# Six tiles of the attention result turned by a 16-bit-plane DMA in place of TensorE, in a fused attention and MLP block

## The chip, the cores and the metric

The kernel runs on one core of a Trainium2 chip. The metric is the device time of one execution in microseconds, lower being better. Times are given as the median of several runs. Beside them there is one profiled execution, whose span is somewhat shorter than the time, since the time also holds what lies around the span.

## The reference

One transformer block on a sequence of 2048 rows of 512 numbers, in float32. The first half is layer norm, one product that gives q, k and v, attention of 32 heads of 16 numbers over a dilated local window (row s looks at rows s, s-2, ..., s-14), and a product with `wo`. The second half is layer norm and an MLP with a hidden layer of 1792, whose activation is the square of relu.

```python
x = A_x
h = x + attention(layernorm(x) @ wqkv) @ wo          # 32 heads, window 8, dilation 2
n = layernorm(h)
r = maximum(n @ w1 + b1, 0)
out = h + (r * r) @ w2 + b2
```

## The kernel before

**Precision.** TensorE multiplies in a reduced float32 form. To keep float32's accuracy, each operand is split in a high part (`hi`, a rounding copy on ScalarE, line 141) and a low part (`lo`, the difference, line 144, on VectorE or GpSimd), and each product is made of three: high by high, low by high, high by low. `mm3` (line 224) issues them as 12 matmuls of 512 columns.

**Tiles and passes.** A tile is 128 rows by 512 numbers. There are 16 tiles, in four groups of four; tile t is in group t // 4. Two neighbouring tiles share one attention output `o_t[s]`, s = t // 2, a buffer of 128 x 2 x 512 out of three that have the tag "o". A first phase makes q, k and v of all tiles and attention and `wo` of group 0. Then the main loop makes three passes, u = 0, 1, 2. In each, TensorE does the MLP of group u, in slots p = 0 to 16: `mlp1` of hidden block p (12 matmuls, line 224), then `mlp2` of the block three slots back (line 808). Into the same slots go the steps of the next group: transposes of the attention result, the `wo` product, and transposes of the normed h. After the loop the MLP of group 3 runs in another form (line 731).

**The order around the change.** The order is written out by hand. Tables at the head of the file give the slot in which each of the four tiles of the next group has its steps; in the third pass the last two tiles are one slot earlier:

```python
LH = 3, 4, 10, 11     # load h
OP = 6, 7, 12, 13     # o_T: transpose the attention result
WP = 8, 9, 13, 14     # the wo product
HP = 15, 15, 16, 16   # h_T: transpose the normed h
```

What a slot starts on TensorE is issued first. Then `end_slot` runs the chores that are due (`at(0, ...)` is due in this slot, `at(1, ...)` in the next), then lets attention run on (`pump`), then runs the late chores (`after`). Each engine takes its instructions in this order. All loads and stores are issued by SyncE, in one queue, and a transfer that must wait holds up those behind it.

**Attention** is a generator, `stream`, which issues VectorE's products and sums (lines 335, 346, 369) and GpSimd's sums over the window, the last of which writes `o` (line 403). It reads windows of k and v (line 243) and q (line 256) from HBM, loaded two steps ahead. `pump` issues attention until the estimated VectorE time has caught up with the estimated TensorE time; `pump(until=s)` issues it until `o_t[s]` is complete.

**The steps of a tile.** `o_T(t)` pumps until its attention is complete, has TensorE transpose four 128x128 blocks into a PSUM bank (`transposes`, line 199), and puts the high part `oh` on ScalarE and the low part `ol` on VectorE among the chores of the same slot. For the third tile of a group both lie in one buffer `ohl` with the tag "o"; otherwise each is a "row", one of 15 buffers that h, r, rl, hn, raw weights and others share. `wo_product(t)` uses `oh` and `ol`, and puts four steps behind itself: the sum with h and its statistics on VectorE (`h_add`, line 577) in the same slot, then the norm on ScalarE, the bias on GpSimd (line 587) and the spill of h to HBM, one to three slots later.

In the loop there are two PSUM banks, taken in turn, for `mlp1`, `wo` and transposes alike. ScalarE empties the bank of `mlp1` with the first step of `hidden` (line 784), a chore of the slot after.

Of the kernel before, what the change touches and what calls it, by code (L numbers as in the profile page):

```python
# [7 lines left out]

F32 = mybir.dt.float32
F32R = mybir.dt.float32r  # L10
AF = mybir.ActivationFunctionType
ALU = mybir.AluOpType
X = mybir.AxisListType.X
# [2 lines left out]
P = 128  # L16
KB = D // P
FB = F // P
R = 4
RI = 2  # L20
# [7 lines left out]
NEG = -4.0e9  # L28
ROWS = 15
LAG = 3  # L30
SLOW = 1.01, 1.12, 1.08
DELAY = 3
WJ = 2
# [1 line left out]
OT = 4, 5, 10, 12  # L35
WO = 7, 9, 13, 15
HT = 20, 20, 21, 23
W2 = (18,)
LH = 3, 4, 10, 11
OP = 6, 7, 12, 13  # L40
WP = 8, 9, 13, 14
HP = 15, 15, 16, 16
UP = 14, 14, 15, 15
HL = (14, 0), (14, 1), (15, 0), (15, 1)
# [8 lines left out]
def block_kernel(ctx, tc, x, wqkv, wo, w1, b1, w2, b2, out):  # L53
    nc = tc.nc
# [3 lines left out]
    att = ctx.enter_context(tc.tile_pool(name="att", bufs=2))  # L58
# [27 lines left out]

    big_h = wpool.tile([P, 3 * KB, D], F32R, name="big_h")
    big_l = wpool.tile([P, 3 * KB, D], F32R, name="big_l")
    wq_h, wq_l = [t.rearrange("p (k c) n -> p k (c n)", k=KB) for t in (big_h, big_l)]
    wo_h = wpool.tile([P, KB, D], F32R, name="wo_h")  # L90
    wo_l = wpool.tile([P, KB, D], F32R, name="wo_l")
    w1_h = wpool.tile([P, KB, F], F32R, name="w1_h")
    w1_l = wpool.tile([P, KB, F], F32R, name="w1_l")
    w2_h, w2_l = {}, {}

    def row(name, shape=(P, D), dt=F32):
        return work.tile(list(shape), dt, name=name, tag="row", bufs=ROWS)
# [8 lines left out]
    def at(delta, fn, *a):  # L106
        due.setdefault(now["slot"] + delta, []).append((fn, a))
# [61 lines left out]
    def act_stats(key, src):  # L169
# [4 lines left out]
        scrap = row("scrap")  # L174
        nc.scalar.activation(scrap, src, AF.Identity, accum_out=nm[:, 0:1])
        nc.scalar.activation(nm[:, 1:2], nm[:, 0:1], AF.Identity, scale=-1.0 / D)
# [30 lines left out]
    def hi_T(tr, h_dst):  # L207
        for d, src in parts(tr, h_dst):
            hi(d, src)

    def lo_T(tr, h_dst, l_dst):
        for (d, src), h in zip(parts(tr, l_dst), h_dst):
            lo(nc.vector, d, src, h)
            dve(0.16 + 0.53 / len(h_dst))
# [16 lines left out]
    o_t = {}  # L231
# [177 lines left out]
    def pump(until=None):  # L409

        while (done[until] < G) if until is not None else (now["dve"] < now["pe"]):
            todo = sums[:]
            sums.clear()
            t = next(stream, "end")
            for a in todo:
                add_up(*a)
            if t == "end":
                now["dve"] = 1e9
                return
            if t is None:  # L420
                now["dve"] = max(now["dve"], now["pe"])
                return
            dve(t * SLOW[min(now['sub'] + 1, 2)])

# [126 lines left out]
    hs, hn = {}, {}  # L551
    oT = {}
# [9 lines left out]
    def o_T(t):  # L562
        s, j = divmod(t, RI)
        pump(until=s)
        tr = transposes(o_t[s][:, j, :])
        if t % R == RI:

            ohl = att.tile([P, 2, KB, P], F32R, name="ohl", tag="o", bufs=3)
            oT[t] = ohl[:, 0], ohl[:, 1]
        else:  # L570
            oT[t] = row("oh", (P, KB, P), F32R), row("ol", (P, KB, P), F32R)
        at(0, hi_T, tr, [oT[t][0]])
        at(0, lo_T, tr, [oT[t][0]], [oT[t][1]])

    def h_add(t, ps):
        h = hs[t]
        nc.vector.tensor_tensor(out=h, in0=ps, in1=h, op=ALU.add)
        dve(0.7)
        norm_stats(t, h)
# [16 lines left out]
    def wo_product(t, slots):  # L596
# [4 lines left out]
        for n, (fn, a) in zip(slots, ((h_add, (t, ps)), (h_norm, (t,)), (add_b2, (t,)),  # L601
# [5 lines left out]
    hh, hl = [[big_l[:, n:n + 2].rearrange("p k (i c) -> p k i c", i=R) for n in ns]  # L607
              for ns in ((0, 3), (6, 9))]

    def h_T(t):  # L610
        if t // R == R - 1:
            return last_h_T(t)
        tr = transposes(hn.pop(t), "mm")
        i = t % R
        hs_, ls_ = [a[:, :, i] for a in hh], [a[:, :, i] for a in hl]
        if len(turn["mm"].tags) > 2:
            at(0, hi_T, tr, hs_)
        else:
            due.setdefault(now["slot"], []).insert(0, (hi_T, (tr, hs_)))
        at(0, lo_T, tr, hs_, ls_)  # L620
# [7 lines left out]
    last_tr, banks = {}, {}  # L628
# [260 lines left out]
    for n in range(16):  # L889
        gp, t = divmod(n, 4)  # L890
# [27 lines left out]
    def first_phase(t0):  # L918
        def chores(m):
            if t0 + 3 < 16:  # L920
                if m in (0, 2):
                    at(0, x_stats, t0 + 2 + m // 2)

                early = t0 == 12
                if m + early in (6, 7):
                    at(0, x_norm, t0 - 4 + m + early)
                if m in XT[early]:
                    x_T(t0 + 2 + XT[early].index(m))
            if t0 + 5 < 16 and m in (6, 9):
                at(0, load_x, t0 + 2 + m // 3)  # L930
            if jobs and m % 3 == 0:
                at(0, weight_job)
            k = t0 // 2 * 12 - 72 + m
            if k == 19:
                dve(HOLD)
            for t in range(R):
                if k == OT[t]:
                    at(0, load_h, t)
                    o_T(t)
                if k == WO[t]:  # L940
                    wo_product(t, (1, 3, 4, 6))
                    now["pe"] += 2.73
                if k == HT[t]:
                    h_T(t)
            if k in W2:
                at(0, load_w2, W2.index(k))

        def half(m):
            end_slot(1.37)
            chores(m)  # L950

        for n in range(6):
            chores(2 * n)
            qkv_of(t0 + n % 2, n // 2, lambda: half(2 * n + 1))
            end_slot(1.37)
# [41 lines left out]
    for u in range(R - 1):  # L997
        now["sub"] = u
        first, end = u == 0, False
        fs = list(range(FB)) if first else [*sorted(place), 12, 13]  # L1000
        fs += [f for f in range(12) if f not in fs and (u < 2 or f not in ENDS)]
        fs += ENDS if u == 2 else []
        need = [] if first else [f for f in fs if f < 12 and f not in place]
        acc = [psum.tile([P, D], F32, name="acc", tag=tag) for tag in ("acc0", "acc1", "tr0", "tr1")]
        js = range(R)


        todo, halves = {}, {}
        for i in js:
            t = R * (u + 1) + i  # L1010
            if not end:
                a = i // 2 if u == 2 else 0
                for p, *what in ((LH[i] - a, at, 0, load_h, t), (OP[i] - a, o_T, t),
                                 (WP[i] - a, wo_product, t, (0, 1, 2 + 3 * a, 3 + 3 * a))):
                    todo.setdefault(p, []).append(what)
                p, h = (HP[i], i % 2) if u < 2 else HL[i]
                (todo, halves)[h].setdefault(p, []).append((h_T, t))
            todo.setdefault(UP[i], []).append((at, 0, unspill, R * u + i))
        if u == 2:
            for p, *what in ((12, at, 0, t_load, 0), (12, at, 0, t_load, 1), (13, after, 0, t_sums, 0),  # L1020
                             (13, after, 0, t_sums, 1), (13, at, 1, t_split, 0),
                             (14, after, 0, t_split, 1)):
                todo.setdefault(p, []).append(what)

        def half(p):
            run(due)
            for fn, *a in halves[p]:
                fn(*a)

        for p in range(FB + LAG):  # L1030
            more = 0.0
            if p == FB:
                run(due)
                dve(HOLD)
            if u < 2 and p == FB - 2:
                dve(HOLD)
            for fn, *a in sorted(todo.get(p, []), key=lambda x: x[0] is wo_product):
                fn(*a)
                more += 2.73 if fn is wo_product else 0.0
            if p < FB:  # L1040
                mlp1(u, fs[p])
                more += 2.73
                if first:
                    at(0, split_w2, p)
                    if p + 1 < FB:
                        load_w2(p + 1)
            q = p - LAG
            if q >= 0:
                f = fs[q]
                mlp2(u, f, acc, js, q == 0, q == FB - 1,  # L1050
                     (lambda: half(p)) if p in halves else None)
                more += 2.74
                if f < 12 and (need or first and p < FB - LAG):
                    free.append(place.pop(f))
                    if need:
                        at(1, fetch, need.pop(0))
            end_slot(more)
        for i in js:
            at(u // 2, finish, R * u + i, acc[i])
# [48 lines left out]
    h = hs[S // P - 1]  # L1108
# [34 lines left out]
```

## Time and profile before

| | |
|---|---|
| time, median of 3 runs | 514.47 us (514.29 to 515.16) |
| the profiled execution: its span | 513.0 us |
| TensorE matmul busy | 506.4 us, 99% |
| VectorE busy | 376.7 us, 73% |
| GpSimd busy | 350.0 us, 68% |
| ScalarE busy | 256.2 us, 50% |
| first phase | 0 to about 160 us |
| main loop, three passes | about 160 to 436 us |
| the last group's MLP | about 436 to 513 us |

Times in profile lines are microseconds from the start of the span unless they are marked as nanoseconds. PE is TensorE, PEld its weight loads, DVE is VectorE, ACT is ScalarE, POOL is GpSimd and SPq is SyncE's queue. In a line of a timeline stand start, duration, engine, line, operation, output and input with their shapes, the number of instructions, and in brackets the idle time before it and what ended it. A group's line ends with its busy time, the mean of one instruction in nanoseconds, and the idle time before. A line of waits has the total, how often, and the longest. A line of DMA issues has the count, the size, and the median time from issue to landing.

### The profile page before, as it was taken

The page shows a single profiled execution, that of the slowest core. Times are in us where ns is not written, and L with a number is a line of the kernel's source. Part 1 is how long each engine was busy: PE and PEld are TensorE (multiplying, and loading weights), DVE is VectorE, ACT ScalarE, POOL GpSimd, SP SyncE. Part 2 cuts the span into 40 slices and gives each one's busy share as a digit, 9 for nine tenths or more (in the row PEclk, how much of TensorE's full clock was granted, in tenths as well). Part 3 has the DMA queues.
Part 4 walks back from the last instruction along what each step waited for, and adds up shares of the span by engine and source line. Part 5 has one row for each costly group of instructions (what it writes and reads, how often), then busy time and mean ns, then how long its engine had stood idle before and what let it go on. Part 6 is the DMA issues. An engine that isn't in the chain of part 4 may idle for free.

```text
span 513.0 us, 7625 instructions
## 1 busy us (share of the span) xinstructions
PE 506.4 (99%) x2508; PEld 429.3 (84%) x2508; DVE 376.7 (73%) x524; ACT 256.2 (50%) x498; POOL 350.0 (68%) x430
## 2 busy tenths in 40 slices
PE   7999999999999999999999999999999999999997
PEld 6999788888888888888888888888888888989996
DVE  5489799988998798976889799778984035742333
ACT  4634687767424763463364334336432525666542
POOL 4714888894885895896778759676889544685520
PEclk9999999999999999999999999999999999999999
DMA  9677989889677895685487537557632352454112
GB/s 265 193 221 188 271 283 315 275 274 278 196 234 201 291 299 173 175 232 180 129 266 229 163 94 231 174 160 257 219 94 65 106 159 84 142 145 145 63 41 82
DMA packets 88239, 97.37 MB, mean 190 GB/s; under 512 B 8328, under 2 KB 56712, under 8 KB 88200
## 3 DMA queue, kind: packets, MB, share of 16 engines
q1 hardware_dynamic: 87256, 96.37, 61.4%
q10 hardware_dynamic: 944, 0.52, 0.3%
q8 instruction: 19, 0.31, 0.3%
q14 instruction: 20, 0.16, 0.1%
HBM read 72.65 MB, written 24.25 MB: 189 GB/s over the span
## 4 chain that ended last, share of the span: by engine, by line
PE 92%; POOL 3%; DMA 2%; DVE 1%; issue 1%; ACT 1%; SPq 0%; POOLq 0%; ACTq 0%
PE mm L224 45%; PE acc L808 29%; PE wo L224 9%; PE mm L731 6%; PE tr L199 4%; DMA wraw<-in_A_wqkv_dram 1%; DMA qkv_d<-y 1%; POOL pr L403 1%; POOL h L587 1%; POOL tl L144 0%; PE half L831 0%; SPq L432 0%; POOL wo_l L144 0%; DVE pr L346 0%; DVE ex L369 0%
## 5 line engine op out<-in xcount | busy, mean ns | idle before, releaser
L403 POOL TENSOR_TENSOR pr<-pr 128x512 f32<-128x512 f32 (+1 forms) x128 | 132.1, 1032 | 51.2 <-DVE pr L346 45.7
L224 PE MATMUL mm<-big_l,w_h 128*128 128x512 f32 x336 | 89.5, 392 | 0.0
L346 DVE TENSOR_TENSOR pr<-ex,v 128x1024 f32<-128x1024 f32 x64 | 78.0, 1221 | 11.6 <-POOL o L403 7.6
L335 DVE TENSOR_TENSOR pr<-qp,k 128x1024 f32<-128x1024 f32 x64 | 76.8, 1201 | 5.7 <-ACT qp L264 5.7
L369 DVE TENSOR_REDUCE ex<-pr 128x64 f32<-128x1024 f32 x64 | 78.4, 1225 | 1.8
L224 PEld LDWEIGHTS mm<-big_l,w_h 128*128 128x128 f32 x336 | 62.3, 188 | 12.8 <-DVE ol L144 0.2
L144 POOL TENSOR_TENSOR rl<-r,rh 128x512 fp32r<-128x512 f32 x42 | 55.4, 1318 | 22.5 <-ACT rh L141 22.4
L224 PE MATMUL mm<-big_h,xl 128*128 128x512 f32 (+1 forms) x208 | 55.9, 379 | 0.2 <-DVE xl L144 0.2
L224 PE MATMUL mm<-big_h,xh 128*128 128x512 f32 (+1 forms) x208 | 53.5, 378 | 0.7 <-ACT xh L141 0.7
L784 ACT ACTIVATE r<-mm,b_sb 128x512 f32<-128x512 f32 x42 | 28.8, 686 | 47.9 <-PE mm L224 46.1
L224 PE MATMUL mm<-big_l,xh 128*128 128x512 f32 (+1 forms) x208 | 52.7, 375 | 0.0
L808 PE MATMUL acc<-big_l,rh 128*128 128x512 f32 x190 | 52.7, 391 | 0.0
L808 PE MATMUL acc<-big_h,rh 128*128 128x512 f32 x190 | 52.3, 392 | 0.0
L808 PE MATMUL acc<-big_h,rl 128*128 128x512 f32 x190 | 51.8, 390 | 0.0
L493 ACT COPY y<-mm 128x512 f32<-128x512 f32 (+1 forms) x52 | 28.6, 552 | 40.0 <-PE mm L224 30.1
L224 PE MATMUL mm<-big_l,w_l 128*128 128x512 f32 x168 | 45.0, 390 | 0.0
L224 PEld LDWEIGHTS mm<-big_h,xh 128*128 128x128 f32 x208 | 37.6, 188 | 7.0 <-ACT xh L141 1.7
L224 PEld LDWEIGHTS mm<-big_l,xh 128*128 128x128 f32 x208 | 38.2, 188 | 6.0
L224 PEld LDWEIGHTS mm<-big_h,xl 128*128 128x128 f32 x208 | 37.2, 188 | 5.7 <-DVE xl L144 0.6
L808 PEld LDWEIGHTS acc<-big_h,rl 128*128 128x128 f32 x190 | 35.7, 188 | 7.5
L808 PEld LDWEIGHTS acc<-big_l,rh 128*128 128x128 f32 x190 | 35.4, 188 | 7.3
L808 PEld LDWEIGHTS acc<-big_h,rh 128*128 128x128 f32 x190 | 34.8, 188 | 6.5
(148 smaller groups left out, 879.8 us busy)
## 6 DMA issues: line engine op xcount, KB each, us to landing
k<-qkv_d SPq DMA_DIRECT2D x48, 288.0 KB, 2.8
v<-qkv_d SPq DMA_DIRECT2D x48, 288.0 KB, 4.0
qkv_d<-y SPq DMA_DIRECT2D x18, 512.0 KB, 4.3
big_l<-w2l_d SPq DMA_DIRECT2D x24, 256.0 KB, 3.1
xt<-in_A_x_dram SPq DMA_DIRECT2D x16, 256.0 KB, 4.3
q<-qkv_d SPq DMA_DIRECT2D x32, 128.0 KB, 3.0
h<-in_A_x_dram SPq DMA_DIRECT2D x16, 256.0 KB, 4.1
h_d<-h SPq DMA_DIRECT2D x16, 256.0 KB, 4.1
```

Source lines behind the costliest of these rows:

```text
L144: eng.tensor_tensor(out=dst, in0=src, in1=h, op=ALU.subtract)
L199: nc.tensor.transpose(tr[:, k, :], src[:, k * P:(k + 1) * P], ident)
L224: nc.tensor.matmul(ps, l(k), r(k), start=(n == 0), stop=(n == 3 * KB - 1))
L335: nc.vector.tensor_tensor(out=pr.rearrange("p i w h d -> p i w (h d)"), in0=qps["now"][:, j % 2].unsqueeze(2).to_broadcast([P, RI, W, GC]) ...
L346: nc.vector.tensor_tensor(out=p2, in1=vwin, op=ALU.mult, in0=e1[:, :, :, j * GH:(j + 1) * GH].unsqueeze(4).to_broadcast([P, RI, W, GH, DH]))
L369: nc.vector.tensor_reduce(out=lf[:, :, :, j * GH:(j + 1) * GH], in_=pr, axis=X, op=ALU.add)
L403: nc.gpsimd.tensor_tensor(out=dst, in0=p2[:, :, :w], in1=p2[:, :, w:2 * w], op=ALU.add)
L493: nc.scalar.copy(y[:, :, t % RI * GC:(t % RI + 1) * GC], ps[:, :j * GC].rearrange("p (j c) -> p j c", j=j))
L587: nc.gpsimd.tensor_tensor(out=h, in0=h, in1=b2_sb, op=ALU.add)
L731: nc.tensor.matmul(ps, sta[y][:, k], mov[x][:, k], start=(first and q == 0), stop=(last and q == len(terms) - 1), skip_group_check=True)
L784: nc.scalar.activation(r, ps, AF.Relu, bias=b1_sb[:, f:f + 1])
L808: nc.tensor.matmul(acc[j], l[:, j * P:(j + 1) * P], w[f], start=(first and n < len(js)), stop=(last and n >= len(terms) - len(js)))
```

## The change

In each pass, the first two tiles of the next group (tiles 4, 5, 8, 9, 12 and 13, the tuple `OV`) are no longer transposed by TensorE. The other tiles are. Three chores in three successive slots take the place of `o_T`:

1. `o_split`, in the slot of `OP`: ScalarE copies the tile, seen as 16-bit integers, into a row buffer `pl`, first all lower halves of the numbers, then all upper halves: two planes of 512 16-bit values.
2. `turn_dma`, one slot later: SyncE issues a transposing DMA of the eight 128x128 blocks of `pl`. It writes into the bytes of the attention output from which the tile came.
3. `o_join`, one slot later again: ScalarE puts the halves of each number together, out of the attention output's bytes back into `pl`. Then ScalarE makes the high part and VectorE the low part, from `pl` in SBUF and not from PSUM.

The `wo` product of these tiles, and the four steps behind it, move one slot later (`WP`). The same functions are there for the normed h, but the tuple `HV` that would use them is empty, and so they are never called. The branch on `OV` in the first phase never applies, since group 0 has no tile in it.

```diff
+U16 = mybir.dt.uint16
...
+OV = (4, 5, 8, 9, 12, 13)
+HV = ()
...
-WP = 8, 9, 13, 14
+WP = 9, 10, 13, 14
...
+    planes = {}
+
+    def halves_of(a):
+        return a.bitcast(U16).rearrange("p (n two) -> p two n", two=2)
+
+    def two_planes(a):
+        return a.bitcast(U16).rearrange("p (two n) -> p two n", two=2)
+
+    def turn_split(key, src):
+
+        planes[key] = src, row("pl")
+        nc.scalar.copy(two_planes(planes[key][1]), halves_of(src))
+
+    def turn_dma(key):
+        src, pl = planes[key]
+        nc.sync.dma_start_transpose(
+            src.bitcast(U16).rearrange("p (n c) -> p n c", c=P), pl.bitcast(U16))
+
+    def turn_join(key):
+        src, pl = planes[key]
+        nc.scalar.copy(halves_of(pl).rearrange("p two n -> p n two"),
+                       two_planes(src).rearrange("p two n -> p n two"))
+        planes[key] = pl.rearrange("p (k c) -> p k c", k=KB)
+
+    def o_split(t):
+        s, j = divmod(t, RI)
+        pump(until=s)
+        turn_split(("o", t), o_t[s][:, j, :])
+
+    def o_join(t):
+        turn_join(("o", t))
+        tr = planes.pop(("o", t))
+        if t % R == RI:
+            ohl = att.tile([P, 2, KB, P], F32R, name="ohl", tag="o", bufs=3)
+            oT[t] = ohl[:, 0], ohl[:, 1]
+        else:
+            oT[t] = row("oh", (P, KB, P), F32R), row("ol", (P, KB, P), F32R)
+        hi_T(tr, [oT[t][0]])
+        lo_T(tr, [oT[t][0]], [oT[t][1]])
...
             if not end:
                 a = i // 2 if u == 2 else 0
-                for p, *what in ((LH[i] - a, at, 0, load_h, t), (OP[i] - a, o_T, t),
+                o0 = OP[i] - a
+                if t in OV:
+                    turned = [(o0, at, 0, o_split, t), (o0 + 1, at, 0, turn_dma, ("o", t)),
+                              (o0 + 2, at, 0, o_join, t)]
+                else:
+                    turned = [(o0, o_T, t)]
...
+                for p, *what in ((LH[i] - a, at, 0, load_h, t), *turned,
                                  (WP[i] - a, wo_product, t, (0, 1, 2 + 3 * a, 3 + 3 * a))):
                     todo.setdefault(p, []).append(what)
```

More of the change, by code (lines that the diff above doesn't have):

```diff
@@ L37 @@
 HT = 20, 20, 21, 23
+OK = (-6, -2, 4), (-5, -1, 5), (3, 6, 10), (4, 7, 12)
+HK = (12, 15, 18), (14, 16, 19)
 W2 = (18,)
@@ L573, in o_T, with h_split, h_parts @@
         at(0, lo_T, tr, [oT[t][0]], [oT[t][1]])
+    planes = {}
[29 more added lines that the diff above has]
+        lo_T(tr, [oT[t][0]], [oT[t][1]])
+    def h_split(t):
+        turn_split(("h", t), hn.pop(t))
+    def h_parts(t):
+        i = t % R
+        tr = planes.pop(("h", t))
+        if t // R == R - 1:
+            last_tr[i] = tr
+            split_last(i, tr)
+            return
+        hs_, ls_ = [a[:, :, i] for a in hh], [a[:, :, i] for a in hl]
+        hi_T(tr, hs_)
+        lo_T(tr, hs_, ls_)
     def h_add(t, ps):
@@ L938, in chores @@
                     at(0, load_h, t)
-                    o_T(t)
+                    if t not in OV:
+                        o_T(t)
+                if t in OV and k in OK[t]:
+                    at(0, (o_split, lambda t: turn_dma(("o", t)), o_join)[OK[t].index(k)], t)
+                if t in HV and k in HK[t]:
+                    at(0, (h_split, lambda t: turn_dma(("h", t)),
+                           lambda t: turn_join(("h", t)))[HK[t].index(k)], t)
                 if k == WO[t]:
@@ L943, in chores @@
                 if k == HT[t]:
-                    h_T(t)
+                    (at(0, h_parts, t) if t in HV else h_T(t))
             if k in W2:
@@ L1012, in block_kernel @@
                 a = i // 2 if u == 2 else 0
-                for p, *what in ((LH[i] - a, at, 0, load_h, t), (OP[i] - a, o_T, t),
+                o0 = OP[i] - a
[4 more added lines that the diff above has]
+                    turned = [(o0, o_T, t)]
+                if t in HV:
+                    h0 = WP[i] - a + 2
+                    turned += [(h0, at, 0, h_split, t), (h0 + 1, at, 0, turn_dma, ("h", t)),
+                               (h0 + 2, at, 0, turn_join, ("h", t))]
+                for p, *what in ((LH[i] - a, at, 0, load_h, t), *turned,
                                  (WP[i] - a, wo_product, t, (0, 1, 2 + 3 * a, 3 + 3 * a))):
@@ L1016, in block_kernel @@
                 p, h = (HP[i], i % 2) if u < 2 else HL[i]
-                (todo, halves)[h].setdefault(p, []).append((h_T, t))
+                if t in HV:
+                    todo.setdefault(p, []).append((at, 0, h_parts, t))
+                else:
+                    (todo, halves)[h].setdefault(p, []).append((h_T, t))
             todo.setdefault(UP[i], []).append((at, 0, unspill, R * u + i))
```

## The prediction

> **What bounds the kernel now.** I read the busy shares first, then windows over the stretches of the main loop that the change touches.
>
> ```profile
> PE 506.4 (99%) x2508; PEld 429.3 (84%) x2508; DVE 376.7 (73%) x524; ACT 256.2 (50%) x498; POOL 350.0 (68%) x430
> 184.00:226.00 42.00, 42.00 (x191) 34.77 (x190) 37.68 (x46) 21.20 (x37) 33.24 (x37) 1.00 0.68 204
> 276.00:317.00 41.00, 41.00 (x186) 33.96 (x185) 35.75 (x42) 17.34 (x31) 29.52 (x37) 1.00 0.53 156
> 367.00:403.00 36.00, 36.00 (x165) 29.72 (x164) 21.63 (x26) 14.74 (x24) 30.05 (x37) 1.00 0.34 103
> ```
>
> The first row is the page's, the others are the windows, one for each pass of the loop (PE, PEld, DVE, ACT, POOL busy, granted clock, DMA share, GB/s). TensorE has no gap in them, at full clock: whatever leaves its queue there shortens the run, if nothing comes late. VectorE stands second, 37.68 of 42 us in the first stretch and 35.75 of 41 in the second, but only 21.63 of 36 in the third. ScalarE has half its time free.
>
> **What is removed.** Two tiles in each of three passes, four transposes each: 24 transposes on TensorE. Matmul records overlap, so I price a tile by starts, in the chain of work that ended last.
>
> ```profile
> 215.63 2.72 PE mm L224 x12
> 218.35 2.72 PE acc L808 x12
> 221.07 2.72 PE mm L224 x12
> ...
> 369.50 0.44 PE tr L199 x4
> 369.94 2.77 PE mm L224 x12
> 372.71 2.72 PE acc L808 x12
> ```
>
> A slot without a transpose is 221.07 - 215.63 = 5.44 us. With one it is 0.44 + 2.77 + 2.72 = 5.93, so a tile costs 0.49 and six cost 2.94 us. This is the whole gain that can be had, 0.57% of the run.
>
> **What is added on ScalarE and VectorE.** Per tile: a split copy, a join copy, and a high part and a low part that now read SBUF instead of PSUM.
>
> ```profile
> L141 ACT CAST th<-traw 128x1024 fp32r<-128x1024 f32 x7 | 7.3, 1050 | 4.9 <-POOL traw L702 4.9
> L141 ACT CAST rh<-r 128x512 fp32r<-128x512 f32 x56 | 34.8, 622 | 2.2
> L141 ACT CAST oh<-tr 128x512 fp32r<-128x512 f32 x12 | 7.0, 586 | 8.5 <-PE tr L199 8.5
> L144 DVE TENSOR_TENSOR ol<-tr,oh 128x512 fp32r<-128x512 f32 x12 | 8.3, 690 | 10.3 <-ACT oh L141 10.1 <-POOL w_l L144 0.2
> L144 DVE TENSOR_TENSOR big_l<-raw,big_h 128x512 fp32r<-128x512 f32 x8 | 6.9, 866 | 2.5 <-ACT big_h L141 2.5
> ```
>
> A copy moves 1024 16-bit values a partition. No such copy is in the trace; the cast of 1024 elements takes 1.05 us and that of 512 (the same bytes) 0.62. I take 1.05, by element, since the strides are odd; the ends are 0.62 and 2.10. With the high part at 0.62 for 0.59, a tile puts 2.13 us on ScalarE, six put 12.8 us. In the first stretch it has 42 - 21.2 = 20.8 us free for 4.3, so this is hidden by its idle time. If that cover were gone, a delay would reach TensorE through the evacuation at line 784. VectorE pays 0.87 - 0.69 = 0.18 per tile, 1.1 us in all, in idle time too.
>
> **What is added on the queue and the DMA engines.** Six transposing transfers of 256 KB, each issued by SyncE one slot after the split.
>
> ```profile
> k<-qkv_d SPq DMA_DIRECT2D x48, 288.0 KB, 2.8
> qkv_d<-y SPq DMA_DIRECT2D x18, 512.0 KB, 4.3
> ...
> 194.94 0.32 SPq L989 DMA_DIRECT2D w2l_d<-big_l  x1
> 197.46 0.32 SPq L243 DMA_DIRECT2D k<-qkv_d  x1
> ...
> 201.27 0.38 SPq L989 DMA_DIRECT2D w2l_d<-big_l  x1
> 205.37 0.32 SPq L243 DMA_DIRECT2D v<-qkv_d  x1
> ```
>
> No transposing transfer is in the trace. From below, the time to landing is 2.8 us (288 KB, long pieces); from above I take two 512 KB stores one after the other, 8.6 us, since the pieces here are rows of 128 16-bit values, 256 bytes. My value is the one store, 4.3, nearest in piece size. The issue itself costs SyncE from 0.32 us (a plain issue) up to the whole landing, if the queue is held while pieces are made; I take 2. In pass 1 the issue for tile 4 falls behind the stash at 194.94, for tile 5 behind the one at 201.27, with 2.2 and 3.7 us until the next load leaves. Queued behind it are the window loads k, v and q (lines 243, 256), which VectorE needs two steps later; 2 us of hold is covered by these gaps, 4.3 us would make one load 2.1 us late, still ahead of its use. The transfer waits for the split, issued a slot earlier on ScalarE, so no new wait for SyncE. The 1.5 MB in all go to engines that are 0.34 to 0.68 busy in these stretches.
>
> The Trainium skill, "DMA: Bandwidth & Descriptors", section "Latency and other measured facts", gives a DMA transpose 261 GB/s: an estimate from it is 1.0 us of movement beside about 2 us fixed, 3.0 in all, within my bounds. No run here shows it yet.
>
> **Is the tile there in time?** The new path is split, transfer, join, high, low, with wo one slot later for these two tiles.
>
> ```profile
> 199.15 1.07 PE L224 MATMUL wo<-wo_h,oh 128*128 128x512 f32 x4
> 196.63 0.69 ACT L784 ACTIVATE r<-mm,b_sb 128x512 f32<-128x512 f32 x1
> 198.01 0.62 ACT L141 CAST rh<-r 128x512 fp32r<-128x512 f32 x1
> 202.07 0.69 DVE L577 TENSOR_TENSOR h<-wo,h 128x512 f32<-128x512 f32 x1 [1.71 <-PE wo L224]
> 290.84 0.37 ACT L392 ACTIVATE ex<-ex 128x256 f32<-128x256 f32 x1 [4.93 <-DVE ex L388]
> ```
>
> In pass 1 slot 8 starts at 199.15, with two transposes gone at 198.17, and slot 9, where tile 4's wo now stands, at 198.17 + 5.44 = 203.6. The transfer leaves at 195.3, lands at 199.6; ScalarE reaches the join after the evacuation of slot 7 (196.63 to 198.63), so join to 200.7, high part to 201.3, low part to 202.2. That is 2.3 us early for the high part; the low part is read four matmuls later. TensorE would wait from a landing of 203.6 - 0.62 - 1.05 - 195.3 = 6.6 us on. Tile 5 leaves at 201.65, is ready at about 208.5, and its wo starts at 203.6 + 8.16 = 211.8. The new wait on ScalarE holds the evacuation behind it; that bank is written again 5.44 us after its product ended, so it is the looser limit.
>
> The narrowest place is pass 2, where the exponential at 290.84 held ScalarE for 4.93 us waiting for VectorE. Were it to stay there, the high part would end at 294.9, just when slot 9 starts. But the two low parts that VectorE did before it, and its waits for them, move behind it, so I expect it some 3 us earlier.
>
> VectorE meets the low part at slot 8, at about 200.4 in this trace (1.71 us before 202.07), and waits until 201.3. It waited 1.71 there for wo before: an exchange, not an addition. In slot 9 I expect 1 to 2 us of waiting for tile 5. What this may use up is the lead of attention over the other two transposes, which stay on TensorE:
>
> ```profile
> 223.02 0.47 POOL L403 TENSOR_TENSOR o<-pr 128x128 f32<-128x128 f32 x1
> 226.51 0.44 PE tr L199 x4
> 315.41 0.47 POOL L403 TENSOR_TENSOR o<-pr 128x128 f32<-128x128 f32 x1
> 317.69 0.44 PE tr L199 x4
> 394.33 0.47 POOL L403 TENSOR_TENSOR o<-pr 128x128 f32<-128x128 f32 x1
> 400.38 2.72 PE acc L808 x12
> ```
>
> The last sum of pass 1 ends at 223.5, 3.0 us ahead of the transpose that reads it; in pass 2 it is 1.8, in pass 3 the sums end at 394.8, 8 us ahead of the transpose after 403.1. TensorE running 0.98 us earlier leaves 2.0, 0.8 and over 7. By my values VectorE is neither earlier nor later than before, so TensorE waits nowhere.
>
> **Sum.** 514.47 - 2.94 = 511.5; I add 0.2 for small waits in pass 2: **511.7 us**. The profiled span is 513.0; the 1.5 us around it are the same before and after, so a span of 510.3.
>
> **Rivals.**
>
> *A: VectorE's waits eat the lead.* At a landing of 6 us VectorE waits until 203.0 for tile 4 (0.3 us more than the 2.3 it gives up: 1.71 and the old wait of 0.6 for the transpose) and some 2.5 us more for tile 5. Attention ends 2.8 us later, so TensorE waits 0.8 in pass 1 and 2.0 in pass 2. The gain is used up: 514.3. For it speaks VectorE's load in two passes; against it that its program order lets it make up time wherever it waits for TensorE today.
>
> ```profile
> 188.56 0.69 DVE L144 TENSOR_TENSOR ol<-tr,oh 128x512 fp32r<-128x512 f32 x1 [0.61 <-ACT oh L141]
> 376.94 0.38 SPq L994 DMA_DIRECT2D big_l<-w2l_d  x1
> 284.38 0.38 SPq L994 DMA_DIRECT2D big_l<-w2l_d  x1
> 381.34 2.72 PE wo L224 x12
> 290.48 2.72 PE wo L224 x12
> ```
>
> *B, the slower side: the transfer is late for wo.* It decides from 6 us on. At 8.6 us tile 4 lands at 203.9, its high part is done at 205.6, 2.0 after slot 9 starts; pass 3 (issue 377.3, slot 9 at 381.34 - 0.98 + 5.44 = 385.8) loses 1.8, pass 2 (issue 284.8, slot 9 at 294.9) 0.2. VectorE is held 5 us in each of the first two passes, which costs 1.4 and 3.9 at the transposes that stay. 4.0 + 5.3 - 2.9 = +6.4: 520.9. For it: blocks that move one after the other; against it: 512 KB in 4.3 us. The Trainium skill, "VectorE: DVE Perf Modes", section "The three transpose paths", has 1309 ns for one 128x128 block by DMA; eight in a row would be an estimate of 10.5 us. No run here shows it.
>
> *C: row buffers.* Each tile holds a further buffer of the 15 for three slots, and h one slot longer. A write into a buffer just freed waits for its last reader:
>
> ```profile
> ACT r L784 <- POOL big_l L144: 1.9, 1, 1.9
> ```
>
> So such a wait is there already, once 1.9 us on ScalarE. If each pass met one such wait that TensorE sees, at half of it, 3 x 0.95 would take the gain: 514.4.
>
> *D: no gain at the end.* Where TensorE waits for GpSimd at the end of the last pass, a faster TensorE could find it no earlier.
>
> ```profile
> 440.82 0.74 POOL L759 TENSOR_TENSOR r<-u,p 128x256 f32<-128x256 f32 x1 [8.52 <-DVE u L757]
> PEld mm L731 <- POOL tl L144: 0.3, 1, 0.3
> ```
>
> GpSimd's run to that wait starts at 440.82 after 8.52 us of idling for a sum of TensorE's products, so it moves along. If not: 514.4.
>
> **How the numbers follow.** Forecast 0.58; A 0.18; B 0.10; C 0.09; D and the rest 0.05. What a measurement here tells from no change is 0.2%, 1.03 us: faster is below 513.44. The forecast's own range is 510.9 to 513.0; with A and C up to 515.5 it holds 0.85 of the cases less their tails, so 510.9 to 515.5. Faster: 0.58, and those of A, C and D that keep half the gain, 0.08: 0.66. Within 0.2%: 0.14, most of A, C and D. Slower: B and the bad half of A, 0.20.
>
> **What would show it.** Right: 24 transposes fewer, slots of 5.44 us where 5.93 stood, a landing of 3 to 6 us, no TensorE idle before wo or before the transposes that stay. Wrong: ScalarE waiting for the transfer with its evacuation late, TensorE idle before wo at slot 9 (B), before the third tile's transposes for GpSimd's sums (A), or before a product whose bank ScalarE freed late (C). A landing above 6 us makes the prediction wrong by itself.

## The result, and the profile after

The changed kernel takes 516.14 us (median of 11 runs) against 514.63 us for the kernel before on the same chip (11 runs). The ratio is 1.0027, with a 95% interval of 1.0015 to 1.0038: slower by 0.27%, where 0.54% faster was forecast, and outside the range. The profiled span is 514.5 us against 513.0. Some executions of most of the kernels below were granted a clock of 0.995 to 0.997 in place of 0.999 to 1.0 and took 1 to 3 us longer: the profiles of e4, e5 and e9 are of such executions, and without its four of twelve e5 would stand at a ratio of 0.999.

First the busy shares of the changed kernel, then the windows over the stretches of the three passes (PE, PEld, DVE, ACT, POOL busy, granted clock, DMA share, GB/s).

```profile
PE 504.7 (98%) x2484; PEld 427.7 (83%) x2484; DVE 378.1 (73%) x524; ACT 268.7 (52%) x510; POOL 349.6 (68%) x430
184.00:226.00 42.00, 42.00 (x189) 34.83 (x188) 37.46 (x45) 25.05 (x41) 32.26 (x37) 1.00 0.72 217
276.00:317.00 41.00, 41.00 (x183) 33.97 (x182) 34.98 (x41) 21.13 (x34) 29.44 (x37) 1.00 0.65 175
367.00:403.00 36.00, 36.00 (x160) 29.82 (x160) 24.62 (x30) 15.67 (x25) 29.76 (x36) 1.00 0.45 128
```

TensorE has 24 matmuls less, and no gap in these stretches: where the transposes were taken out, nothing is late. The loss lies behind them. Here are the waits of TensorE's weight loads in the changed kernel, and the same group of waits in the kernel before (total, times, longest).

```profile
PEld tr L204 <- ACT hn L199: 3.2, 2, 2.2
PEld tr L204 <- POOL o L408: 1.6, 1, 1.6
```

```profile
PEld tr L199 <- ACT hn L194: 0.4, 1, 0.4
```

In TensorE's timeline of the changed kernel they stand at these places:

```profile
252.91 0.66 PE L204 MATMUL tr<-ident,hn 128*128 128x128 f32 x4 [1.79 <-ACT hn L199]
319.24 0.33 PE L204 MATMUL tr<-ident,o 128*128 128x128 f32 x1 [1.37 <-POOL o L408]
```

The first is the transpose of the normed h of tile 7, the last step of pass 1 ahead of the next group's MLP. The second is tile 10 in pass 2, the third tile of its group, which TensorE still transposes. The other wait for the normed h is that of tile 11, at the end of pass 2. Together they are 3.2 + 1.6 = 4.8 us, where the kernel before waited 0.4: 4.4 us more. With 2.94 us saved, 1.5 us of loss is left, which is the measured one.

The new path itself did what was expected of it. From the view of the tile `pl` (nanoseconds: lowest, median, highest; then who waited for whom, in us):

```profile
L591 ACT COPY pl<-o x6: 1037/1042/1042, 186.8 to 376.4; 128x1024 uint16<-128x1024 uint16 x6
L595 SPq DMA_TRANSPOSE o<-pl x6: 1237/1369/2152, 193.4 to 382.0; - x6
L600 ACT COPY pl<-o x6: 1162/1168/1177, 197.8 to 388.3; 128x1024 uint16<-128x1024 uint16 x6
L146 ACT CAST oh<-pl x6: 620/621/622, 199.1 to 389.5; 128x512 fp32r<-128x512 f32 x6
DMA to landing us min/median/max: 3.6/4.0/4.4
```

So the question is why attention, which feeds both late steps, came late, although nothing was put on its engines beyond six slightly different low parts.

### The profile page after: what moved, and what is told of

It reads as the page before. It is cut to its first block, busy times and chain, and to the rows that moved or that the text cites. A ratio compares the mean times of both kernels' runs of the same rounds, so it can differ in the third digit from the quotient of the medians.

```text
span 514.5 us, 7605 instructions
## 1 busy us (share of the span) xinstructions
PE 504.7 (98%) x2484; PEld 427.7 (83%) x2484; DVE 378.1 (73%) x524; ACT 268.7 (52%) x510; POOL 349.6 (68%) x430
```

## The experiments

Three theories. *Held*: VectorE waits in its order for the low parts of the turned tiles, and attention behind them is late. *No lead*: the late steps had no lead before either, so what TensorE saves in passes 1 and 2 it waits off. *Clock* (the schedule's own count, not the clock granted to TensorE), formed after the first four runs: `transposes` does not only issue transposes, it also counts them in the schedule's estimate of TensorE's time, and with the call the count went too.

```python
    def transposes(src, banks="tr"):
        ...
        now["pe"] += 0.44
        return tr
```

`pump` issues attention until VectorE's estimated time has caught up with this count. With 0.88 us less in each pass, attention's instructions are issued later in the program, behind other instructions of VectorE, and VectorE, which works in order, stands before them and waits.

Each run is compared with the kernel before on the same chip.

| run | time, us | kernel before, us | ratio, 95% interval |
|---|---|---|---|
| the change | 516.14 | 514.63 | 1.0027 (1.0015 to 1.0038) |
| e1: six tiles not transposed | 519.11 | 515.10 | 1.0074 (1.0058 to 1.0090) |
| e2: the change without the transfer | 516.04 | 515.10 | 1.0018 (1.0008 to 1.0027) |
| e3: pass 3 alone, two tiles | 514.49 | 515.10 | 0.9980 (0.9964 to 0.9996) |
| e4: wo one slot later alone | 515.65 | 515.10 | 1.0008 (0.9998 to 1.0019) |
| e5: the change, 0.44 counted | 514.75 | 515.24 | 1.0007 (0.9990 to 1.0024) |
| e6: the change, 1.5 counted | 515.04 | 515.24 | 1.0002 (0.9991 to 1.0013) |
| e7: before, 0.44 not counted | 521.98 | 515.24 | 1.0130 (1.0116 to 1.0145) |
| e8: path a slot earlier, late low part, 0.44 counted | 512.93 | 515.29 | 0.9951 (0.9939 to 0.9963) |
| e9: pass 3 alone, four tiles | 514.00 | 515.29 | 0.9976 (0.9965 to 0.9987) |
| e10: six tiles not transposed, 0.44 counted | 512.43 | 515.29 | 0.9950 (0.9938 to 0.9962) |
| e11: e8 without the count | 516.40 | 515.33 | 1.0021 (1.0010 to 1.0031) |
| e12: e8 with the low part at once | 514.53 | 515.33 | 0.9980 (0.9967 to 0.9992) |

**e1: the removal alone.**

```diff
-        tr = transposes(o_t[s][:, j, :])
+        if t in (4, 5, 8, 9, 12, 13):
+            tr = o_t[s][:, j, :].rearrange("p (k c) -> p k c", k=KB)
+        else:
+            tr = transposes(o_t[s][:, j, :])
```

> The kernel before, with the transposes of the six tiles left out and nothing put in their place: the high and low parts are taken from the attention result in SBUF, not turned, in the slots of before. It shows what the removal can bring when it costs nothing. Theory 'held' (VectorE is held by the low parts of the turned tiles, so attention is late): nothing holds it here, all of 2.9 us is gained, about 511.7. Theory 'no lead' (the last normed h of passes 1 and 2 came just as TensorE needed it already, because attention's sums on VectorE and GpSimd set its time, so what TensorE saves in these passes it waits off again): only pass 3's 0.98 is gained, about 513.6, with TensorE idle some 1 us before the transposes of the normed h in passes 1 and 2.

Neither: 519.11 us, 4.0 us slower than before, with less work for TensorE, no copies and no transfer. The waits of the weight loads:

```profile
PEld tr L199 <- ACT hn L194: 3.3, 2, 2.3
PEld mm L224 <- ACT r L787: 2.2, 1, 2.2
PEld tr L199 <- POOL o L403: 1.7, 1, 1.7
```

The first and the third row are those of the change, almost to the tenth. So it isn't the new path that makes them, and *held* falls as their cause. *No lead* can at most bring the gain back to nothing, not turn it into a loss of 4 us.

The second row is a wait in pass 3 that the change doesn't have. GpSimd's statistics stand behind a sum of attention, ScalarE waits for them before a normed h, and the evacuation of TensorE's bank stands behind that:

```profile
402.50 2.11 POOL L403 TENSOR_TENSOR pr<-pr 128x512 f32<-128x512 f32 x2
406.52 0.81 ACT L194 ACTIVATE hn<-h,rs 128x512 f32<-128x512 f32 x1 [2.49 <-POOL rs L162]
407.24 0.67 ACT L787 ACTIVATE r<-mm,b_sb 128x512 f32<-128x512 f32 x1
```

The three rows of waits are 7.2 us together, 6.8 more than the 0.4 before; less the 2.9 saved that is 3.9 us, against 4.0 measured.

**e2: no transfer.** `turn_dma` only swaps the two buffers, so that the join puts the planes together again unturned.

```diff
     def turn_dma(key):
-        src, pl = planes[key]
-        nc.sync.dma_start_transpose(
-            src.bitcast(U16).rearrange("p (n c) -> p n c", c=P), pl.bitcast(U16))
+        planes[key] = planes[key][::-1]
```

> The changed kernel with the transposing transfer left out: the split goes into planes, the join puts them together again unturned, slots and ScalarE's copies as in the change. 'held', by the transfer: VectorE's wait of 3.8 us for the first low part of pass 2 shrinks to under 2, and the time falls by 1 to 3 us against the change, to 513 to 515. If the copies and the later wo do it, not the transfer: no fall, 516. 'no lead' alone: not under 513.6.

516.04 us. By the ratios that is 0.5 us under the change, and the two intervals overlap: no fall is shown, and the 1 to 3 us of *held* are not there. VectorE's wait for the first low part of pass 2 did shrink, from 3.81 to 1.67 us, and the time did not follow. The transfer, SyncE's time for it and its landing cost little in the change.

**e3: pass 3 alone.** `OV = (12, 13)`; `WP` as before, plus one slot for the tiles of `OV`.

> The change in pass 3 alone (tiles 12 and 13), passes 1 and 2 as before. Both theories: attention is 8 us ahead there and the last normed h is not set by it, so 0.98 us is gained, 513.6. If the transfer or the copies cost something by themselves there, 514.6 or more.

It came out so within the interval: a ratio of 0.998, 1.0 us (0.2 to 1.9), against 0.98 us expected. Where attention is far ahead, the change gains about what it was priced at.

**e4: wo one slot later.** The kernel before with `WP = 9, 10, 13, 14`.

> The kernel before with nothing but the wo products of the first two tiles of each pass one slot later, as in the change. Both theories: no change within 0.3 us, 514.6. Rival 'later wo': h, its statistics and its bias move into GpSimd's and VectorE's busy slots and delay the normed h of the last tile; then 515 to 516, with TensorE idle before the transposes of the normed h.

0.4 us slower by the ratio, with an interval from no change to 1.0 us. The transposes of the normed h waited 0.5 us, against 0.4 before, and the third tile's not at all: the later wo does not make the two waits of the change.

**e5 and e6: the count.** In the changed kernel:

```diff
         pump(until=s)
         turn_split(("o", t), o_t[s][:, j, :])
+        now["pe"] += 0.44
```

> The changed kernel; the split adds to the schedule's count of TensorE time the 0.44 us that the removed transposes added, so that attention is issued as early among the slots as before. Theory 'clock' (with less TensorE time counted, attention's instructions slid behind waiting ones in VectorE's order, so VectorE idles where it had work): VectorE's order is again near the one of before, the waits before the normed h of pass 1 and before the third tile's transposes of pass 2 shrink to about 1 us each, the time falls by 1 to 2.5 us against the change, to 513.7 to 515. Theory 'new path' (ScalarE's copies, the queue and the join delay attention): no fall, 516.

With 1.5 in place of 0.44:

> As the run before, with 1.5 us in place of 0.44 for each turned tile, so that attention runs ahead of its old place. 'clock': attention gains up to 2 us of lead in each of passes 1 and 2, TensorE's waits there are gone or under 0.5 us, 512 to 513.7. 'no lead' (VectorE and GpSimd have no time left in these passes, whatever the order): no better than the run before, since the lead can't be made. 'new path': 516.

By the intervals neither can be told from the kernel before. The median of e5 lies in the range of *clock*, that of e6 above it; that e6 is no better than e5 is what *no lead* had, which stands until e10. The waits for the third tile are gone and those for the normed h are 0.5 us or none, but others have come. In e5 and then in e6:

```profile
PEld mm L229 <- ACT r L844: 2.4, 1, 2.4
PEld wo L229 <- ACT r L844: 0.7, 1, 0.7
PEld tr L204 <- ACT hn L199: 0.5, 1, 0.5
```

```profile
PEld wo L229 <- DVE ol L149: 1.4, 3, 0.7
PEld wo L229 <- ACT oh L146: 1.1, 3, 0.6
PEld mm L229 <- DVE ol L149: 0.7, 1, 0.7
PEld wo L229 <- ACT r L844: 0.6, 1, 0.6
PEld mm L229 <- ACT r L844: 0.6, 1, 0.6
```

Once attention is in time, the new path shows. In e5 it is ScalarE's evacuation in pass 1: VectorE had stood 5.49 us for the high part of tile 5, later ScalarE stood 6.55 us for VectorE's input to an exponential, and the evacuation came behind it; that the first made the second was not followed through. In e6, with more attention put ahead, it is the parts of the turned tiles themselves, which wo now waits for. The profile of e5 took 517.11 us, 2.4 above its median: right behind the wait, TensorE's matmuls took 1.57, 1.91 and 1.54 us for four where 1.07 is usual, so what the wait cost in the other executions is not shown.

**e7: the count alone.** The kernel before, with all its transposes:

```diff
         tr = transposes(o_t[s][:, j, :])
+        if t in (4, 5, 8, 9, 12, 13):
+            now["pe"] -= 0.44
```

> The kernel before with all its transposes, only that the schedule's count of TensorE time is 0.44 us less for each of the six tiles. Nothing that the chip executes is removed or added; the order of attention among the slots alone moves. 'clock': slower by 0.5 to 2 us, with TensorE idle before the normed h of pass 1 or the third tile of pass 2, in the places of the change. 'new path' and 'no lead': within 0.3 us of before.

521.98 us. Nothing is removed or added on the chip, and the kernel is 1.3%, some 6.7 us, slower, with the same waits:

```profile
PEld tr L199 <- ACT hn L194: 3.3, 2, 2.3
PEld mm L224 <- ACT r L786: 2.2, 1, 2.2
PEld tr L199 <- POOL o L403: 1.7, 1, 1.7
```

That is *clock*, though far more than the 0.5 to 2 us expected. The waits are 6.8 us more than the 0.4 before, which accounts for the loss. The orders of VectorE, ScalarE and GpSimd in e7 are those of e1, instruction by instruction; the two differ by the transposes alone: 521.98 - 519.11 = 2.87 us. They ran on different chips; by the ratios it is 0.56%, 2.9 us, give or take 1.1.

**e10: the removal with the count.** e1 with `now["pe"] += 0.44` in the branch without transposes.

> The first run again (the six tiles not transposed, their parts taken unturned from the attention result), now with the removed transposes still counted in the schedule, so that VectorE's order is that of before. It leaves the transposing out. 'clock': what TensorE saves is gained except where the normed h had no lead before: 511.7 to 513.6, and 5.5 to 7.4 us under the first run, though the chip does the same work. 'no lead' in full: only pass 3's 0.98, 513.6 to 514. Theory 'the removal itself hurts' (fewer bank turns, other buffers): 519 as in the first run.

512.43 us. The orders of VectorE, ScalarE and GpSimd are those of the kernel before, and the difference is 515.29 - 512.43 = 2.86 us (2.0 to 3.2 by the interval). The two pairs price the 24 transposes alike, once in the good order and once in the bad one. *No lead* falls with it: with the old order the saving is gained. The wait for the normed h is 0.4 us as before, although TensorE comes earlier, since what feeds it comes earlier too. GpSimd's sum ahead of the statistics at the end of pass 1, at 240.76 us in the kernel before, in e10:

```profile
239.74 2.10 POOL L403 TENSOR_TENSOR pr<-pr 128x512 f32<-128x512 f32 x2 [3.48 <-DVE pr L346]
```

**e8, e11 and e12: a version with a gain, and two of its three parts.**

```diff
-                o0 = OP[i] - a
+                o0 = OP[i] - a - (t in OV)
...
         turn_split(("o", t), o_t[s][:, j, :])
+        now["pe"] += 0.44
...
-        lo_T(tr, [oT[t][0]], [oT[t][1]])
+        after(0, lo_T, tr, [oT[t][0]], [oT[t][1]])
```

> The changed kernel with 0.44 counted as before, with split, transfer and join one slot earlier, and with the low part among the late chores of its slot, so that VectorE meets it after a slot's attention. It is meant to have neither the slid order nor the new path's waits. 'clock' with the new path's waits as the rest of the loss: 512 to 513.5, no TensorE wait on ScalarE's evacuation and none before wo. If the rest is not these waits: 514.7 as with 0.44 alone.

512.93 us, a ratio of 0.9951: faster than both kernels, and within the forecast of the better case. It computes the whole block. e11 takes only the count out of it, e12 only the late low part; the earlier slot was not taken out by itself.

> The last version with a gain (split, transfer and join one slot earlier, the low part among the late chores) with the 0.44 us not counted. 'clock': the slid order comes back with its waits before the normed h or the third tile, 514.5 to 516.5, 2 us or more above the version with the count. If the earlier path is what brought the gain: 512.5 to 513.5, as with the count.

> The same version with the count, but with the low part right behind the high part, as in the change, so that VectorE meets it before the slot's attention. If VectorE's wait for the low part is a cost of its own: 513.5 to 515, with TensorE waiting in pass 1 or 2. If the count and the earlier slot are enough: 512.5 to 513.2.

Without the count 516.40 us: the same code, with 6 x 0.44 us less in an estimate, is 0.7% slower, and the two waits are back.

```profile
PEld tr L204 <- ACT hn L199: 3.2, 2, 2.3
PEld tr L204 <- POOL o L408: 1.4, 1, 1.4
```

With the low part at once 514.53 us, 0.3% above e8, with 1.6 us of waiting for ScalarE's evacuation. VectorE waited 4.22, 2.03 and 3.01 us for high parts of turned tiles in passes 1 and 2, and in e8 for none. So *held* is a cost too, of about 1.5 us, once the order is right; with the slid order it hardly shows (e11 is 0.06% better than the change, within the intervals).

**e9: pass 3 alone, four tiles.** e3 with `OV = (12, 13, 14, 15)`; tiles 14 and 15 split in slot 10, their wo in slot 13.

> The change in pass 3 alone, for all four tiles 12 to 15, passes 1 and 2 as before; tiles 14 and 15 split in slot 10, when attention is done, joined in slot 12, their wo in slot 13. No attention is left in VectorE's order behind slot 10, so nothing can slide: four transposes' worth, 4 x 0.49 = 2.0 us, is gained, 512.7, against 1.0 with two tiles. If ScalarE's copies or the later wo hold the normed h of the last tile: 513.6 to 515.

1.2 us by the ratio, between the two (0.7 to 1.8). The intervals of e3 and e9 overlap, so whether the two further tiles gain anything is open.

## Why the prediction was wrong

**The step that failed** is the first of the change: "What is removed. Two tiles in each of three passes, four transposes each: 24 transposes on TensorE." That is what is removed from the chip. From the program the call of `transposes` is removed, and with it the 0.44 that it adds to the count by which attention is issued. The front part names the count ("`pump` issues attention until the estimated VectorE time has caught up with the estimated TensorE time"), but the prediction put no price on a change to it, and held that "VectorE is neither earlier nor later than before, so TensorE waits nowhere". How one instruction slides can be seen at tile 7 in pass 1. VectorE in the kernel before:

```profile
229.34 1.22 DVE L335 TENSOR_TENSOR pr<-qp,k 128x1024 f32<-128x1024 f32 x1
232.92 1.22 DVE L346 TENSOR_TENSOR pr<-ex,v 128x1024 f32<-128x1024 f32 x1 [2.37 <-POOL o L403]
...
234.66 0.68 DVE L144 TENSOR_TENSOR ol<-tr,oh 128x512 fp32r<-128x512 f32 x1
235.67 0.69 DVE L577 TENSOR_TENSOR h<-wo,h 128x512 f32<-128x512 f32 x1 [0.33 <-PE wo L224]
```

VectorE in the changed kernel:

```profile
229.25 1.21 DVE L340 TENSOR_TENSOR pr<-qp,k 128x1024 f32<-128x1024 f32 x1
...
232.69 0.69 DVE L149 TENSOR_TENSOR ol<-tr,oh 128x512 fp32r<-128x512 f32 x1 [1.21 <-ACT oh L146]
234.78 0.69 DVE L636 TENSOR_TENSOR h<-wo,h 128x512 f32<-128x512 f32 x1 [1.40 <-PE wo L229]
...
236.33 1.21 DVE L351 TENSOR_TENSOR pr<-ex,v 128x1024 f32<-128x1024 f32 x1
```

The weighting of v (`pr<-ex,v`) stood ahead of the low part and of the sum with h; now it stands behind both and comes 3.41 us later. VectorE idles 1.21 + 1.40 us before the two; in the old order it idled about as long, 2.37 + 0.33 us, but most of it ahead of the weighting. GpSimd's sums of attention follow VectorE's products, and the statistics of the normed h stand behind the sums in GpSimd's order. GpSimd in the kernel before, then in the changed one:

```profile
240.76 2.11 POOL L403 TENSOR_TENSOR pr<-pr 128x512 f32<-128x512 f32 x2 [3.50 <-DVE pr L346]
249.95 0.23 POOL L158 TENSOR_SCALAR rs<-mv 128x1 f32<-128x1 f32 x1
```

```profile
241.60 2.11 POOL L408 TENSOR_TENSOR pr<-pr 128x512 f32<-128x512 f32 x2 [1.34 <-DVE pr L351]
250.76 0.23 POOL L163 TENSOR_SCALAR rs<-mv 128x1 f32<-128x1 f32 x1
```

The sum starts 0.84 us later, and 0.81 us later come the statistics of tile 7, on which its normed h and its transpose wait. TensorE, 0.98 us earlier by then, waits the 1.79 us of the timeline above. So the term of the sum that failed is TensorE's waiting, put at 0.2 us for small waits in pass 2: it was 4.4 us more than before.

**The place not looked at.** I checked the lead of attention over the third tile's transposes (3.0 and 1.8 us) and not that of the normed h over its own. The row of 0.4 us in the kernel before says that this lead was nothing. It is the larger of the two waits. By itself that cost nothing, since in the old order the normed h comes earlier together with TensorE (e10); it left no room for the slid order.

**Rival A** named one of the right places, the third tile of pass 2, and a wait of the right size there (2.0 against 1.6 us), but as its cause a landing of 6 us. e2, without any transfer, has the wait too. So it was right by place alone.

**What held.** The saving: 2.94 us forecast, 2.87 and 2.86 in the two pairs. The copies: 1.04 and 1.17 us against 1.05. The issue: 1.24 to 2.15 us against 2. The landing: 4.0 us against 4.3. Slot 9 of pass 1 started its wo at 203.69 against 203.6, and nothing waited before a wo. The low part from SBUF took 0.69 us in the median, not 0.87. I added no hold of the queue to the landing: tile 8's transfer began to be issued at 285.71 and its join could start at 291.71, 6.0 us later; TensorE waited before no wo all the same. In the narrow place of pass 2 the exponential came behind the high part and not ahead of it, so the high part was done at 293.53 us, 2.1 before its wo at 295.61.

**Rivals B, C and D.** B did not come: no wo waited. C, a write that waits for a buffer's last reader, may be behind ScalarE's late evacuation in e5, where it waited 0.28 us for GpSimd's low part of a weight just before TensorE's wait; that it is the buffer was not tried, and 0.28 is a small part of the 2.4 us. D did not come either: the passes' delay of 1.3 us, from 435.88 to 437.15 us at the last stage's first products, was not made up there: the end moved from 513.0 to 514.5 us.

**Left open.** The waits account for what the count alone costs, 6.7 us in e7 and some 3.5 in e11 against e8, but which slid instruction makes which wait was followed only for tile 7. Why the change lacks the wait in pass 3 that e1 and e7 have is open too, and so is what the earlier slot adds in e8.

## What to carry to other kernels

When a schedule is made by counting time, an edit that takes out an instruction also takes out its count, and everything that is placed by the count moves: before a part is priced, look up what else its call does, and compare the order of each engine's instructions. The cheapest test is to change the count alone and leave the work. And a lead is to be checked for every step that ends a stage, not only for the one that the edit touches: a wait of 0.4 us in the profile is a lead of nothing, which costs nothing as long as that step moves along with TensorE, and all of any delay when it doesn't.

## What the runs showed of the hardware

A transposing transfer of 256 KB between two SBUF buffers held SyncE's queue for 1.24 to 2.15 us (median 1.37), where a plain load of k or v took 0.32 and one of q 0.43 in the median, and landed after 3.6 to 4.4 us by the view of the tile `pl`. Plain transfers of the same size in the changed kernel, between HBM and SBUF, had medians from 3.0 to 5.5 us, so the landing is no longer than theirs.

ScalarE's copies of 1024 16-bit values a partition took 1.04 us (to planes) and 1.17 (from planes), by element and not by byte: 512 32-bit values, the same bytes, took 0.62.

The 24 transposes of 128 x 128 cost 2.87 and 2.86 us in the two pairs of kernels, 0.12 us each, while the profile's record of a single one lasts 0.27 us, so the records overlap.
